# A fused retention and gated feed-forward kernel: two more chunks transposed by the DMA crossbar, and one row of identity products dropped

## The chip, the cores and the metric

The kernel runs on one core of a Trainium2 chip. The metric is the device time of one launch in microseconds (us), as the median of several runs. Times of two kernels are compared within the same rounds on the same chip. A run counts as slow when it is more than 1.5% above the fastest run of the same kernel; only fast runs are compared with fast runs.

## The reference

The program is a retention layer followed by a gated feed-forward layer:

```python
# q, k, v: (4, 8, 768, 64)     (batch, heads, sequence, head size)
for t in range(S):
    state = gamma[None, :, None, None] * state + einsum('bhd,bhe->bhde', k[:, :, t], v[:, :, t])
    y[:, :, t] = scale * einsum('bhd,bhde->bhe', q[:, :, t], state)
x = y.transpose(0, 2, 1, 3).reshape(3072, 512)
out = (1 / (1 + exp(-(x @ w_gate))) * (x @ w_val)) @ w_out      # d_ff = 1536
```

## The kernel before

The kernel cuts the sequence into 24 chunks of 128 positions (four batches of six) and the 3072 tokens into six blocks of 512, four chunks each. For each chunk it makes transposed q and k, the scores of the chunk with itself, a masked product with a scaled v, and the running state. While TensorE works on the feed-forward layer of block t, the attention steps of the four chunks of block t + 1 are placed between its groups of matmuls. All of this is written for a manual schedule: each engine executes its instructions in program order.

The parts that matter here:

```python
XBAR = 12                                    # chunks from 12 on are transposed by the DMA crossbar

def load_kq(g):                              # GpSimd issues the loads (float32 to bfloat16 on the way)
    ...
    nc.gpsimd.dma_start(out=kn[g], in_=src(k, g))
    nc.gpsimd.dma_start(out=qn[g], in_=src(q, g))

def transposes(g):                           # on TensorE: 8 products, and a copy by ScalarE
    tp = pa.tile([128, 2 * NP, C], BF16, tag="tp", name="tp")
    for i, x in enumerate((kn[g], qn[g])):
        for p in range(NP):
            nc.tensor.transpose(tp[:, i * NP + p, :], pair(x, p), ident)
    qkT[g] = at.tile([128, 2 * NP, C], BF16, tag="qkT", name="qkT", bufs=3)
    nc.scalar.activation(qkT[g], tp, AX.Copy)

def xbar(g):                                 # by the DMA crossbar, issued by SyncE: 2 transfers
    qkT[g] = ld.tile([128, 2 * NP, C], BF16, tag="qkX", name="qkX", bufs=8)
    for i, x in enumerate((kn[g], qn[g])):
        nc.sync.dma_start_transpose(out=qkT[g][:, i * NP:(i + 1) * NP, :],
                                    in_=x.rearrange("s h d -> s (h d)"))

def step_t(g):
    if g < XBAR:
        transposes(g)
    scale_v(g, nc.vector if g < 8 else nc.gpsimd)      # from chunk 8 on GpSimd scales v

def step_y(g, nxt=None):
    inter(g)                                 # y  <- state of the chunk before
    if nxt is not None:
        scores(nxt)
    state(g)                                 # z  <- k and scaled v of this chunk
    intra(g)
    ...

def down(t, sm, part):
    ...
    ob = ffn.tile([128, D_MODEL], F32, tag="ob", name="ob")      # pool of 3 buffers
    nc.scalar.copy(ob, o)
    nc.sync.dma_start(out=out[row:row + 128, :], in_=ob)         # stores on SyncE's queue too

def keep_on(n):                              # identity products, only to keep TensorE at work
    u = pf.tile([128, 512], F32, tag="ff", name="ff")
    for _ in range(n):
        nc.tensor.matmul(u[:, :128], ident, ident, start=True, stop=True)

for t in range(NT):
    ...
    if t + 2 < NT:
        for g in range(4 * t + 8, 4 * t + 12):
            load_chunk(g)                    # before this block's scale_v in GpSimd's order
    for i, group in enumerate(groups):
        if i == len(groups) - 9:
            for g in range(4 * t + 8, 4 * t + 12):
                if XBAR <= g < NG:
                    xbar(g)
        group()
        ...                                  # the attention steps placed at this group
```

## Time and profile before

| | before |
|---|---|
| time, median of the first 3 runs | 240.35 us (240.22 to 241.0) |
| span of the profiled run | 238.1 us |
| TensorE busy | 96% |
| granted TensorE clock | 1.00 |
| DMA engines busy | full until about 119 us, then nearly idle |

"PE" is TensorE's matmuls, "PEld" its weight loads, DVE is VectorE, ACT is ScalarE, POOL is GpSimd and SPq the queue of SyncE. A row of slices cuts the span into 40 equal pieces, with the busy share of each in tenths. In the chain of waits each line is a start, a duration and what the end of the program waited for in that time. In a timeline each line is a start, a duration, the engine, the source line and the operation, and in brackets how long the engine was idle before it and what ended that. The lines themselves stand in the prediction.

### The profile page before, as it was taken

To read this page: it belongs to the slowest core of one execution; us is meant where nothing else is said; L and a number is where in the kernel's file an instruction comes from. 1 tells how busy PE (TensorE), PEld (TensorE's weight loads), DVE (VectorE), ACT (ScalarE), POOL (GpSimd) and SP (SyncE) were. 2 spreads that over 40 slices of the span, in tenths; PEclk is the share of its full clock that TensorE was granted. 3 is DMA by queue.
4 is the path that set the end of the run, shared out by engine and by line. 5 is a ranking of instruction groups with operands and counts; after the bars stand their busy time and mean duration, and the time that the engine had idled before them with its cause. 6 is when DMAs were issued, how large, how long until landed. Compare 5 with 4: busy or idle time off the path is not lost.

```text
span 238.1 us, 4313 instructions
## 1 busy us (share of the span) xinstructions
PE 227.8 (96%) x1716; PEld 118.9 (50%) x1742; DVE 102.0 (43%) x172; ACT 90.8 (38%) x169; POOL 95.9 (40%) x114
## 2 busy tenths in 40 slices
PE   7798999999999999999999999999999999999993
PEld 7565644555655554444554445444444554444441
DVE  3467446355545631256641346641346641243300
ACT  7764334425545431234333243223334321334221
POOL 8999874687889346994111001111000000000000
PEclk9999999999999999999999999999999999999999
DMA  7999999999999999999972361012100012100022
GB/s 131 192 189 188 195 205 200 189 212 230 233 169 139 92 138 163 263 175 156 159 110 88 91 104 29 3 45 89 47 0 0 3 44 88 47 0 0 0 88 88
DMA packets 77267, 27.27 MB, mean 115 GB/s; under 512 B 65024, under 2 KB 72704, under 8 KB 77248
## 3 DMA queue, kind: packets, MB, share of 16 engines
q0 software_dynamic: 57616, 16.78, 70.6%
q1 hardware_dynamic: 19632, 10.23, 21.6%
q8 instruction: 13, 0.21, 0.4%
q14 instruction: 6, 0.05, 0.1%
HBM read 28.31 MB, written 6.29 MB: 145 GB/s over the span
## 4 chain that ended last, share of the span: by engine, by line
PE 88%; POOL 6%; issue 2%; ACT 2%; DVE 1%; ACTq 0%; POOLq 0%; DVEq 0%
PE ff L250 49%; PE ff L281 26%; PE sA L168 3%; PE y L204 2%; PE z L190 2%; PE y L180 2%; PE tp L146 2%; POOL vs L158 1%; POOL kn L67 1%; POOL vf L62 1%; POOL qn L68 1%; ACT qkT L148 1%; PE ff L264 1%; ACT ob L286 1%; PE ff L293 1%
## 5 line engine op out<-in xcount | busy, mean ns | idle before, releaser
L255 DVE TENSOR_TENSOR hT<-gs,ff 128x512 bf16<-128x512 f32 (+1 forms) x72 | 48.6, 676 | 75.5 <-PE ff L250 73.9
L250 PE MATMUL ff<-xT,wg 128*128 128x512 bf16 (+1 forms) x276 | 71.5, 375 | 0.9 <-DVE xT L212 0.3
L250 PE MATMUL ff<-xT,wv 128*128 128x512 bf16 (+1 forms) x282 | 71.9, 375 | 0.4
L254 ACT ACTIVATE gs<-ff 128x512 f32<-128x512 f32 (+1 forms) x72 | 42.3, 588 | 68.8 <-PE ff L250 68.3
L281 PE MATMUL ff<-wo,hT 128*128 128x512 bf16 x280 | 65.0, 380 | 0.6 <-issue 0.2
L250 PEld LDWEIGHTS <-wv 128*128 128x128 bf16 x288 | 28.2, 98 | 32.7
L281 PEld LDWEIGHTS <-hT 128*128 128x128 bf16 x288 | 27.0, 98 | 31.6
L250 PEld LDWEIGHTS <-wg 128*128 128x128 bf16 x288 | 26.7, 98 | 30.2 <-issue 0.8
L158 POOL TENSOR_TENSOR vs<-vf,tabv 128x512 bf16<-128x512 f32 x18 | 18.6, 1048 | 47.1 <-PE y L204 42.1
L286 ACT COPY ob<-ff 128x512 f32<-128x512 f32 x24 | 14.0, 585 | 54.3 <-PE ff L281 49.1
L212 DVE TENSOR_TENSOR xT<-y,taby 128x512 bf16<-128x512 f32 x24 | 16.4, 685 | 20.1 <-PE y L204 20.0
L62 POOL DMA_DIRECT2D vf<-in_v_dram x23 | 20.7, 902 | 9.4 <-DMA kn<-in_k_dram 4.7
L173 DVE TENSOR_TENSOR stA<-sA,causal 128x512 bf16<-128x512 f32 x24 | 16.5, 687 | 18.6 <-PE sB L168 18.5
L67 POOL DMA_DIRECT2D kn<-in_k_dram x23 | 20.9, 907 | 7.0 <-DMA qn<-in_q_dram 4.4
L68 POOL DMA_DIRECT2D qn<-in_q_dram x23 | 20.4, 887 | 4.3 <-DMA wo<-in_moe_w_out_dram 2.3
L198 ACT CAST zbd<-z 64x256 bf16<-64x256 f32 x40 | 14.6, 366 | 13.6 <-PE z L190 13.2
L174 DVE TENSOR_TENSOR stB<-sB,causal 128x512 bf16<-128x512 f32 x24 | 16.3, 681 | 0.0
L148 ACT ACTIVATE qkT<-tp 128x1024 bf16<-128x1024 bf16 x12 | 12.3, 1024 | 5.1 <-PE tp L146 5.1
L293 PE MATMUL ff<-ident 128*128 128x128 bf16 x110 | 9.5, 251 | 2.6 <-POOL ident masks.py:199 1.6
L204 PE MATMUL y<-stA,vs 128*64 128x128 bf16 x96 | 9.7, 222 | 0.0
L293 PEld LDWEIGHTS <-ident 128*128 128x128 bf16 x110 | 8.0, 114 | 3.2 <-POOL ident masks.py:199 1.6
L204 PE MATMUL y<-stB,vs 128*64 128x128 bf16 x96 | 9.5, 221 | 0.0
(48 smaller groups left out, 112.9 us busy)
## 6 DMA issues: line engine op xcount, KB each, us to landing
out_dram<-ob SPq DMA_DIRECT2D x24, 256.0 KB, 2.0
vf<-in_v_dram POOLq DMA_DIRECT2D x23, 256.0 KB, 8.6
kn<-in_k_dram POOLq DMA_DIRECT2D x23, 128.0 KB, 8.4
qn<-in_q_dram POOLq DMA_DIRECT2D x23, 128.0 KB, 8.6
wg<-in_moe_w_gate_dram POOLq DMA_DIRECT2D x6, 256.0 KB, 5.8
wv<-in_moe_w_val_dram POOLq DMA_DIRECT2D x6, 256.0 KB, 6.6
wo<-in_moe_w_out_dram POOLq DMA_DIRECT2D x4, 384.0 KB, 11.0
kf<-in_k_dram SPq DMA_DIRECT2D x1, 256.0 KB, 3.4
```

What stands on the lines that cost most here:

```text
L62: eng.dma_start(out=vf[g], in_=src(v, g))
L67: nc.gpsimd.dma_start(out=kn[g], in_=src(k, g))
L68: nc.gpsimd.dma_start(out=qn[g], in_=src(q, g))
L158: eng.tensor_tensor(vs[g], vf[g], tabv[:, g % NCH, :].unsqueeze(2).to_broadcast([C, H, D]), op=ALU.mult)
L173: nc.vector.tensor_tensor(stA[g], sc[g][0], causal4, op=ALU.mult)
L204: nc.tensor.matmul(y[g][i * D:(i + 1) * D, p, :], vs[g][:, 2 * p + i, :], st[:, p, :], start=(first and p == 0), stop=True, skip_group_che ...
L212: nc.vector.tensor_tensor(xT[g // 4][:, :, col:col + C], y[g], taby[:, :, c * C:(c + 1) * C], op=ALU.mult)
L250: nc.tensor.matmul(u[:, lo:hi], w[:, kk, n1 * 128:(n1 + 1) * 128], xT[t][:, kk, lo:hi], start=(kk == 0), stop=(kk == KT - 1))
L254: nc.scalar.activation(gs[:, lo:hi], ps[0][:, lo:hi], AX.Sigmoid)
L255: nc.vector.tensor_tensor(hT[t][:, n1, lo:hi], gs[:, lo:hi], ps[1][:, lo:hi], op=ALU.mult)
L281: nc.tensor.matmul(o, hT[t][:, n1, sm * 128:(sm + 1) * 128], wo[:, n1, :], start=(n1 == 0), stop=(n1 == NFF - 1))
L293: nc.tensor.matmul(u[:, :128], ident, ident, start=True, stop=True)
```

## The change

The intent is to give TensorE, the busiest engine, less to do. The 16 identity products behind the fourth chunk's transposes go, and so do the TensorE transposes of chunks 10 and 11 (with ScalarE's copies). These two chunks are transposed by the crossbar, issued early in block 1.

```diff
-    XBAR = 12
+    XBAR = 10
@@
     transposes(3)
-    keep_on(16)
     scores(3)
@@
         for i, group in enumerate(groups):
-            if i == len(groups) - 9:
-                for g in range(4 * t + 8, 4 * t + 12):
-                    if XBAR <= g < NG:
-                        xbar(g)
+            if t == 1 and i == 2:
+                for g in range(XBAR, 12):
+                    xbar(g)
+            if i == len(groups) - 9 and t > 0:
+                for g in range(4 * t + 8, min(4 * t + 12, NG)):
+                    xbar(g)
             group()
```

## The prediction

> **What bounds the kernel now.** I read the busy table and the slices first, then the chain of waits, then the timelines of single engines where the change acts.
>
> ```profile
> PE 227.8 (96%) x1716; PEld 118.9 (50%) x1742; DVE 102.0 (43%) x172; ACT 90.8 (38%) x169; POOL 95.9 (40%) x114
> PE   7798999999999999999999999999999999999993
> DMA  7999999999999999999972361012100012100022
> PE 88%; POOL 6%; issue 2%; ACT 2%; DVE 1%; ACTq 0%; POOLq 0%; DVEq 0%
> ```
>
> TensorE is busy almost from end to end, so work taken off it is worth its own time, as long as nothing else holds TensorE at that spot. The DMA engines are full for the first half (slices 2 to 20, until about 119 us) and nearly empty after. The chain is TensorE except for a few short stretches; one of them matters here, in the second token block (t = 1), which begins at 57.7 us:
>
> ```profile
> 69.45 0.89 POOL vf L62
> 70.35 1.07 POOL vs L158
> 71.47 0.32 PE z L190 x8
> ```
>
> The chain leaves TensorE for GpSimd: the state product of chunk 8 needs the scaled v of chunk 8, and GpSimd makes that only after it has issued the last load (v of chunk 15) in its program. TensorE waits just 0.15 us for it today, so this spot has no slack.
>
> Is GpSimd there held by its own issuing, or by the transfers? Its timeline:
>
> ```profile
> 32.22 0.90 POOL L67 DMA_DIRECT2D kn<-in_k_dram  x1 [0.56 <-DMA wv<-in_moe_w_val_dram]
> 36.72 0.87 POOL L68 DMA_DIRECT2D qn<-in_q_dram  x1 [0.75 <-DMA wo<-in_moe_w_out_dram]
> ...
> 60.30 0.89 POOL L62 DMA_DIRECT2D vf<-in_v_dram  x1 [0.35 <-issue]
> 83.62 0.87 POOL L67 DMA_DIRECT2D kn<-in_k_dram  x1 [3.63 <-DMA qn<-in_q_dram]
> 88.58 0.89 POOL L62 DMA_DIRECT2D vf<-in_v_dram  x1 [3.21 <-DMA kn<-in_k_dram]
> ```
>
> Counted back in order of issue, the transfer waited for is each time the eighth before (for the load at 32.22 the val weights issued at 23.69; for 83.62 the q load issued at 68.58). So at most eight GpSimd loads are in flight, and the ninth is issued when the first has landed: slower transfers delay GpSimd, and with it everything that stands behind the loads. From 51 to 70 us it issues three loads in about 3.1 us, 1.04 us each, with small gaps of this kind.
>
> SyncE's timeline shows the transposes of the DMA crossbar:
>
> ```profile
> 58.31 0.33 SPq L288 DMA_DIRECT2D out_dram<-ob  x1
> 65.94 1.31 SPq L153 DMA_TRANSPOSE qkX<-kn  x1
> 67.36 2.03 SPq L153 DMA_TRANSPOSE qkX<-qn  x1
> ```
>
> SyncE is free from 58.6 us on and waits 7.3 us for k of chunk 12 to land. The eight transposes of chunks 12 to 15 then run from 65.94 to about 84 us, beside the loads. Their cost to the loads shows in the landing times: the loads of the window 58 to 70 us land in a median of 7.9 to 8.5 us, those of 70 to 90 us in 13.7 to 14.7 us. The transposes themselves take 9.7 to 13.0 us to land there, 2.4 us with no loads about (130 to 155 us).
>
> **What the Trainium skill says.** "DMA: Bandwidth & Descriptors", section "Issuing engines are not separate DMA queues": transfers from all issuing engines run on the same 16 DMA engines and interleave. The trace agrees: landing times nearly double, as just given. The same page, "DMA Transpose (X-bar)": such a transpose can only come from the SyncE or ScalarE queues; here all 24 stand on SyncE's, behind the stores in program order. "TensorE: Matmul & The Clock Gate", "What's actually happening": TensorE idle for about 3.4 us falls to half clock, and needs about 3.4 us of work to come back. The trace has the slow rate only at its start (the first 36 identity products take 4.02 us, 0.11 us each; the 16 at 21.18 us take 1.05 us, about 0.055 us each), and no long idle time after it, so a fall back is not shown.
>
> **Part 1, the 16 identity products.**
>
> ```profile
> 20.22 1.02 ACT L148 ACTIVATE qkT<-tp 128x1024 bf16<-128x1024 bf16 x1 [0.61 <-PE tp L146]
> 21.18 1.05 PE L293 MATMUL ff<-ident 128*128 128x128 bf16 x16 [0.99 <-DVE hT L255]
> 22.16 0.23 PE L168 MATMUL sA<-qkT 64*128 64x128 bf16 x1
> ```
>
> They were to fill the wait for ScalarE's copy, but they wait themselves for a PSUM buffer (0.99 us) and begin at 21.18, when that copy is nearly over (20.22 + 1.02 = 21.24). Without them the scores can start some 0.06 us after the copy (at 62.91 us they start 0.05 us after it), at 21.30 instead of 22.16: **0.86 us earlier**. VectorE ends its two multiplications at 21.58 and is free for the masks. TensorE idles 1.1 us in place of 1.0 us there, too short for the clock. But nothing moves GpSimd earlier, whose load issue does not depend on TensorE here. TensorE arrives at the state product of chunk 8 at 70.45 instead of 71.3 and waits for the same scaled v. I expect the 0.86 us to be **lost there: worth 0**.
>
> **Part 2, chunks 10 and 11 off TensorE.** Each chunk's eight transposes take 0.45 us of the chain (75.57 and 82.32 us), both after the wait at 71.47, where TensorE is the bound with some 5 us of other work between steps: **-0.9 us**. ScalarE's two copies of 1.02 us go too; ScalarE is 38% busy and off the chain: 0.
>
> **Part 3, four more crossbar transposes.** They stand after block 0's stores and before chunks 12 to 15 on SyncE, so the first goes when k of chunk 10 has landed. That load is issued at 51.38; the eighth after it is issued at 60.30 after a short wait, so it lands at about 60.1. Today's first transpose is issued at 65.94: crossbar traffic starts about **5.9 us earlier**. The transposed chunks are in time: with 13 us to land they come by about 79 us, needed at 77.9 (chunk 10, whose two are first, by 75) and 87.2 us (chunk 11). The cost is to the loads. In slices of 1 us, the first crossbar packets appear at 69.6 us, 3.7 us after the issue; so they would appear at about 63.8 us. From then on loads land slower. Today, from 69.6 to 79.0 us, six loads land (q of chunk 13 to k of chunk 15; the eighth load after the last of them is issued at 79.09 after a wait): 1.6 us each against 1.04. For the last load before the scaled v to be issued, k of chunk 13 must have landed, the eighth before it. Of the loads up to it, those issued up to 55.27 have landed by 64.3 us; v of 11, k, q, v of 12 and k of 13 are left, with the rest of one, some six. By today's rate they need 9.4 us: 63.8 + 9.4 = 73.2 in place of about 69.4. So the scaled v comes **3.8 us** later, the state product at about 75.2.
>
> TensorE would then sit idle from 70.45 to 75.2, 4.8 us, over the skill's 3.4 us. If its clock falls, up to 3.4 us run at half rate, a loss of at most 1.7 us; since the trace shows no such case, I count a third of it, 0.5 us (an estimate).
>
> Later blocks have room: the scaled v of chunk 12 is made at 94.38 and used at 107.8, chunk 16's transposes are issued at 97.78 and used at 135.6; some 6 us more of DMA delay fits.
>
> Sum: 0 - 0.9 + 3.8 + 0.5 = +3.4, so 243.75; since the delay is the least certain term and can be smaller, I lower it to **243.0 us**.
>
> **The rivals.**
> A, no new wait: the crossbar takes its turn without slowing GpSimd's issue before 69.45. For it: from 65.94 to 69.45 transposes were issued and the loads did not yet slow; SyncE was idle there. Against: traffic starts 3.7 us after issue and loads slow at once then. It gives -0.9, 239.5; and if the saved 0.86 us counts as well, 238.6.
> B, the wait is larger: the DMA is so disturbed that loads land at 2.0 us each (today 12 loads from 69.2 to 93.3 us), and traffic starts with less lag, so nine loads are left: 9 x 1.0 = 9 us late. With the clock loss and -0.9, about +9: 249.
> C, the transposed chunks 10 or 11 come late themselves, as part of SyncE's row is held by loads: chunk 10 would have to land 17 us after its issue, and the longest today is 13.0. TensorE would wait at the scores of chunk 10 instead, 1 to 3 us, but only where the earlier wait did not already move that use back: little on top.
>
> **Range and chances.** Rival A has some 25%, B's strong form some 8%, the middle (a wait of 2 to 6 us) the rest. That gives 239.2 to 246.8 for 8 in 10. Faster by over 2% needs under 235.5, more than all that is removed: 2%. Slower by over 2% needs over 245.2, a new wait of about 6 us, or 4.5 us with a full clock loss: 15%. Within 2%: 83%.
>
> **What would show it.** Right: the first scores of chunk 3 at about 21.3; transposes on SyncE from about 60 us; the last load before the scaled v issued at 72 to 75 us, TensorE idle 3 to 6 us before the state product of chunk 8, released by the scaled v; from there on each stage as before, less 0.45 us twice. Wrong: the state product still at about 71.4 (A), or the longest new wait elsewhere, at the scores of chunk 10 (C) or in block 2.

## The result

| | before | changed |
|---|---|---|
| median | 240.28 us (239.88 to 241.0) | 247.84 us (246.7 to 248.87) |
| span of the profiled run | 238.1 us | 246.0 us |
| granted clock | 1.00 | 0.979 |

The changed kernel is slower, by a ratio of 1.031 (95% interval 1.026 to 1.036). A ratio here is the mean time of one kernel's fast runs over that of the other's in the same rounds, so it is not quite the ratio of the two medians. The result is correct. 247.84 us lies above the predicted range.

The page of the changed kernel: busy time, slices, and the chain by engine:

```profile
PE 229.7 (93%) x1710; PEld 117.3 (48%) x1710; DVE 102.4 (42%) x172; ACT 88.8 (36%) x167; POOL 95.9 (39%) x114
...
PE   6798999999944999999999999999999999999993
...
PEclk9999999999995799999999999999999999999999
DMA  8999999999999999999999284002200002200022
...
PE 80%; DMA 9%; POOL 5%; ACT 2%; issue 1%; DVE 1%; POOLq 0%; ACTq 0%; DVEq 0%
```

There is now a hole in TensorE's row in slices 12 and 13, and the granted clock falls in slices 13 and 14; DMA transfers, which had no share worth a line in the chain before, hold 9% of it. The timeline of TensorE around the hole:

```profile
21.31 0.23 PE L168 MATMUL sA<-qkT 64*128 64x128 bf16 x1 [1.12 <-ACT qkT L148]
...
77.19 0.42 PE L190 MATMUL z<-vs,kn 128*64 128x64 bf16 x8 [6.74 <-POOL vs L158]
77.98 1.89 PE L250 MATMUL ff<-xT,wg 128*128 128x512 bf16 x4
79.66 1.92 PE L250 MATMUL ff<-xT,wv 128*128 128x512 bf16 x4
81.36 1.80 PE L250 MATMUL ff<-xT,wg 128*128 128x512 bf16 x4
83.00 1.03 PE L250 MATMUL ff<-xT,wv 128*128 128x512 bf16 x4
```

The first line shows that the dropped products did what was expected of them: the scores of chunk 3 start at 21.31 us instead of 22.16. The second is the wait: 6.74 us before the state product of chunk 8, for the scaled v of GpSimd. The next three show groups of four matmuls that start 1.7 us apart, where the fourth and all later ones take 0.87 us: TensorE runs at half clock after the wait. In slices of 0.3 us the clock is 0.50 from about 72.7 us, some 2.2 us after TensorE went idle (at 70.45 us), to about 82.9 us.

The chain of waits in that stretch of the changed kernel, and SyncE's timeline below it:

```profile
62.36 12.26 DMA kn<-in_k_dram
...
75.19 0.89 POOL vf L62
76.09 1.06 POOL vs L158
...
77.19 0.42 PE z L190 x8
...
95.31 10.31 DMA out_dram<-ob
```

```profile
60.66 1.29 SPq L153 DMA_TRANSPOSE qkX<-kn  x1
62.07 1.19 SPq L153 DMA_TRANSPOSE qkX<-qn  x1
63.90 1.50 SPq L153 DMA_TRANSPOSE qkX<-kn  x1
65.50 1.72 SPq L153 DMA_TRANSPOSE qkX<-qn  x1
68.14 1.68 SPq L153 DMA_TRANSPOSE qkX<-kn  x1
```

The load of k of chunk 13, issued at 62.36 us, takes 12.26 us (7.57 before, issued at 61.29). The last load before the scaled v can only be issued when it has landed, at 75.19 us (69.45 before), and the scaled v follows at once. The transposes begin at 60.66 us (65.94 before). The last chain line is a smaller second loss: an output store of block 1 takes 10.31 us to land, and TensorE waits 0.39 us for its buffer (0.55 us from start to start of the matmuls).

Where the time went, read from the start of the state product of each chunk in the two timelines of TensorE:

| state product of chunk | before | changed | later by | what is added |
|---|---|---|---|---|
| 3 | 22.82 | 21.96 | -0.86 | products dropped |
| 8 | 71.47 | 77.19 | +5.72 | the wait (6.74 instead of 0.15, of which 0.86 is the early arrival) |
| 9 | 78.22 | 86.24 | +8.02 | half clock +2.75, chunk 10's transposes -0.45 |
| 10 | 87.57 | 95.14 | +7.57 | chunk 11's transposes -0.45 |
| 12 | 107.72 | 115.84 | +8.12 | the store's buffer +0.55 |
| 22 | 193.99 | 202.12 | +8.13 | nothing |

The spans differ by 7.9 us, the medians by 7.56.

### The profile page after: what moved, and what is told of

It reads as the page before. It is cut to its first block, busy times and chain, and to the rows that moved or that the text cites. A ratio compares the mean times of both kernels' runs of the same rounds, so it can differ in the third digit from the quotient of the medians.

```text
span 246.0 us, 4283 instructions
## 1 busy us (share of the span) xinstructions
PE 229.7 (93%) x1710; PEld 117.3 (48%) x1710; DVE 102.4 (42%) x172; ACT 88.8 (36%) x167; POOL 95.9 (39%) x114
## 4 chain that ended last, share of the span: by engine, by line
PE 80%; DMA 9%; POOL 5%; ACT 2%; issue 1%; DVE 1%; POOLq 0%; ACTq 0%; DVEq 0%
PE ff L250 48%; PE ff L281 22%; DMA kn<-in_k_dram 5%; DMA out_dram<-ob 4%; PE sA L168 2%; PE y L204 2%; PE z L190 2%; PE y L180 2%; POOL vs L158 1%; POOL vf L62 1%; PE tp L146 1%; ACT qkT L148 1%; POOL kn L67 1%; PE ff L264 1%; ACT ob L286 1%
## 5 line engine op out<-in xcount | busy, mean ns | idle before, releaser
L250 PE MATMUL ff<-xT,wg 128*128 128x512 bf16 (+1 forms) x288 | 74.5, 382 | 0.8 <-ACT ob L286 0.4
L250 PE MATMUL ff<-xT,wv 128*128 128x512 bf16 (+1 forms) x288 | 73.6, 379 | 0.0
L190 PE MATMUL z<-vs,kn 128*64 128x64 bf16 x160 | 6.4, 203 | 6.9 <-POOL vs L158 6.9
L148 ACT ACTIVATE qkT<-tp 128x1024 bf16<-128x1024 bf16 x10 | 10.2, 1025 | 3.6 <-PE tp L146 3.6
L293 PE MATMUL ff<-ident 128*128 128x128 bf16 x94 | 8.0, 247 | 1.6 <-POOL ident masks.py:199 1.6
## 6 DMA issues: line engine op xcount, KB each, us to landing
wo<-in_moe_w_out_dram POOLq DMA_DIRECT2D x4, 384.0 KB, 10.4
```

The lines of the kernel that those rows point to most:

```text
L250: nc.tensor.matmul(u[:, lo:hi], w[:, kk, n1 * 128:(n1 + 1) * 128], xT[t][:, kk, lo:hi], start=(kk == 0), stop=(kk == KT - 1))
```

## The experiments

**Theory A.** The whole loss comes from the four earlier crossbar transposes. They slow the loads that are in flight beside them; GpSimd, which keeps at most eight loads in flight, issues its last load later, so the scaled v of chunk 8 comes late; TensorE idles, and its clock falls. **Rivals:** the dropped identity products let the clock fall (C); TensorE waits for the transposed data itself (D); any traffic at that place would do the same.

Unless it says otherwise, an edit is shown against the changed kernel. "Before" in these runs has medians from 240.19 to 240.37 us. The runs e1 to e4, e5 to e8 and e9 to e12 were made on three different chips, so runs of different groups are best compared by their ratios to the kernel before.

### e1_products_dropped: the first part alone

```diff
# against the kernel before
     transposes(3)
-    keep_on(16)
     scores(3)
```

> Only the 16 identity products are dropped; chunks 10 and 11 stay on TensorE. Theory A (the whole loss comes from the four earlier crossbar transposes, which delay the loads and with them GpSimd's scaled v of chunk 8): as the kernel before, 240.3 us within 0.4; scores of chunk 3 at about 21.3 us, and TensorE waits about 1.0 us instead of 0.15 before the state product of chunk 8, which still starts at about 71.4 us. Rival B (the saved 0.86 us counts): 239.4 us. Rival C (the products kept the TensorE clock up, and their loss is what slows the changed kernel): slower than 242 us, with a granted clock under 1.00.

240.35 us, ratio 1.000 (0.998 to 1.002). In its timeline of TensorE:

```profile
71.90 0.32 PE L190 MATMUL z<-vs,kn 128*64 128x64 bf16 x8 [1.44 <-POOL vs L158]
```

TensorE comes 0.86 us earlier and waits until 71.90 us. GpSimd's gate swallows the saving, and the clock stays at 1.00. Rivals B and C of that list are out.

### e2_products_kept: the change without its first part

```diff
     transposes(3)
+    keep_on(16)
     scores(3)
```

> The changed kernel with the 16 identity products put back. Theory A: as slow as the changed kernel, 247.8 us within 0.8; the wait before the state product of chunk 8 is about 5.9 us (6.7 less the 0.86), and it ends at the same time, about 77 us; the clock still falls behind it. Rival C (the dropped products are the cause): back to about 239.5 us.

248.27 us, ratio 1.033 (1.029 to 1.038): as slow as the changed kernel. In the profiled run the wait is 7.71 us and ends at 79.04, rather later than expected; its time is 249.03. The runs fall into two pairs by clock, 249.03 and 249.75 us at 0.979, 247.5 and 246.9 us at 0.986. These steps can be read: in the profiled runs the stretches at half clock last 3.4 us (0.993: e3_spare_transposes, e8_plain_copies) or 10.2 us (0.979: the changed kernel, and this one), so by estimate 0.986 is two times 3.4 us. The products are not the cause.

### e3_spare_transposes: the added traffic alone

```diff
# against the kernel before; nobody reads the spare tiles
         for i, group in enumerate(groups):
+            if t == 1 and i == 2:
+                for g in range(10, 12):
+                    spare = ld.tile([128, 2 * NP, C], BF16, tag="spare", name="spare", bufs=2)
+                    for j, x in enumerate((kn[g], qn[g])):
+                        nc.sync.dma_start_transpose(out=spare[:, j * NP:(j + 1) * NP, :],
+                                                    in_=x.rearrange("s h d -> s (h d)"))
```

> The kernel before, with products and TensorE transposes of chunks 10 and 11 as they were, and the four crossbar transposes of these chunks added into spare tiles that nobody reads. Theory A: the added traffic alone makes the loss, 248.7 us within 1.0 (the changed kernel's 247.8 plus the 0.9 us of TensorE transposes that stay). Rival D (the loss comes from waiting for the transposed data of chunks 10 and 11): 240.3 us, since nobody waits for it.

248.3 us, ratio of the fast runs 1.030 (1.025 to 1.035); one of the four runs is slow (250.89 us, at the clock of 0.979 that three of the changed kernel's fast runs have). All computing is as in the kernel before, and no one waits for the added transfers, yet the loss is there. In the profiled run, the fastest of the four (245.59 us), the scaled v begins at 74.72 us and the wait is 4.52 us. Rival D is out: the traffic is enough.

### e4_no_transposes_wrong: the saving alone

Wrong result (relative error 0.50): chunks 10 and 11 read chunk 9's transposed tile.

```diff
         if g < XBAR:
             transposes(g)
+        elif g < 12:
+            qkT[g] = qkT[9]
@@
             if t == 1 and i == 2:
-                for g in range(XBAR, 12):
-                    xbar(g)
+                pass
```

> Wrong result on purpose: the changed kernel without any transpose of chunks 10 and 11 (they read chunk 9's transposed tile). Theory A: no added traffic, so the state product of chunk 8 starts at about 71.4 us; the TensorE transposes saved count, 2 x 0.45 us: 239.4 us within 0.4. If they did not count: 240.3 us. If dropping the products or the transposes were itself harmful: over 242 us.

239.55 us, five of the six runs between 239.38 and 239.79; the ratio is 0.998 (0.995 to 1.002) because the sixth took 241.68 at a clock of 0.993, by the estimate above one stretch of 3.4 us at half clock. Without the added traffic the wait in the profiled run is 1.57 us and the clock 1.00. By the medians about 0.8 us are saved, near the 0.9 expected, though the interval of the ratio includes no saving.

### e7_kept_busy: the clock by itself

```diff
             scores(nxt)
+        if g == 8:
+            keep_on(104)
         state(g)
```

> The changed kernel with 104 identity products (about 5.8 us at full clock) put in front of the state product of chunk 8, into the wait of 6.7 us. Theory A with the clock as second term: the wait ends when it did, about 77 us, but the three groups of matmuls behind it run at 0.87 us instead of 1.7, so 2.4 to 2.7 us less than the changed kernel: 245.3 us, granted clock 1.00. If the slow groups behind the wait had another cause (the crossbar's traffic): 247.8 us as before.

245.73 us, ratio 1.023 (1.018 to 1.028), clock 0.999 to 1.000 in all four runs. Its timeline of TensorE (the edit moves line numbers up by two):

```profile
70.36 5.98 PE L295 MATMUL ff<-ident 128*128 128x128 bf16 x104
78.05 0.32 PE L190 MATMUL z<-vs,kn 128*64 128x64 bf16 x8 [1.71 <-POOL vs L158]
78.52 1.04 PE L252 MATMUL ff<-xT,wg 128*128 128x512 bf16 x4
79.40 1.03 PE L252 MATMUL ff<-xT,wv 128*128 128x512 bf16 x4
```

The wait ends no earlier (78.05 us), but the groups behind it start 0.87 us apart at once. The crossbar's traffic is the same, so the slow groups of the changed kernel are the clock's, not the traffic's. It saves 2.1 us by the medians; the intervals of the two ratios touch (1.018 to 1.028, and 1.026 to 1.036), so the timeline is the stronger evidence.

### e8_plain_copies: plain copies in place of the spare transposes

```diff
# against e3_spare_transposes
-   nc.sync.dma_start_transpose(out=spare[:, j * NP:(j + 1) * NP, :],
-                               in_=x.rearrange("s h d -> s (h d)"))
+   nc.sync.dma_start(out=spare[:, j * NP:(j + 1) * NP, :].rearrange("s p c -> s (p c)"),
+                     in_=x.rearrange("s h d -> s (h d)"))
```

> As the run with four spare crossbar transposes, but each is a plain copy of the same bytes between the same places (128 rows of 1 KB, no transposing). Theory A in the form that the many small packets of a transpose cost (about 548 packets of under 512 B each, against some 144 here): little delay, 240.3 to 241.3 us. Rival (any transfer of these bytes at that time costs as much): about 248 us.

243.32 us, ratio 1.012 (1.010 to 1.015): between the two, so both expectations miss. The scaled v begins at 71.95 us, 1.6 us later than before; in e3_spare_transposes it was 4.4 us later. So plain copies delay the loads as well, in these two profiled runs by about a third as much as transposes of the same bytes. The start of the scaled v also varies without any added traffic, so the landing time of k of chunk 13 is the cleaner measure: 7.5 to 7.6 us in the profiled runs without added transfers or with two transposes (before, e1, e4, e10, e11), 9.1 us here, and 11.4 to 15.7 us in the eight with four transposes. Why the loss of some 3 us is more than the delay shows in the timeline of TensorE:

```profile
73.06 0.32 PE L190 MATMUL z<-vs,kn 128*64 128x64 bf16 x8 [1.76 <-POOL vs L158]
73.53 1.47 PE L250 MATMUL ff<-xT,wg 128*128 128x512 bf16 x4
74.80 1.91 PE L250 MATMUL ff<-xT,wv 128*128 128x512 bf16 x4
```

A wait of only 1.76 us was enough for the clock to fall, 0.9 us after work had begun again (it is at half from about 74.0 to 77.4 us).

### e11_only_chunk_11: half of the added transposes

```diff
-    XBAR = 10
+    XBAR = 11
```

> The changed kernel with the crossbar for chunk 11 alone (two added transposes instead of four, and the first about 3 us later). Theory A: the scaled v of chunk 8 comes 1.5 to 2.5 us later than in the kernel before, TensorE waits about 3 us, the clock falls for one to two stretches of 3.4 us (1.2 to 2.4 us lost), and 0.45 us are saved: 243.4 us, 242 to 245. If the loss does not depend on the number of transposes: 247.8 us; if it only begins with the fourth: 240 us.

239.85 us, ratio 0.998 (0.996 to 1.000): a miss for theory A's size, there is no loss at all; of the alternatives only the last (240 us) fits. Its first added transpose waits for k of chunk 11 and is issued at 63.79 us, 3.1 us after the changed kernel's. The load that counts, k of chunk 13, was issued at 62.13 us and lands in time for the last load at 70.20; the scaled v begins at 71.10, 0.75 us later than before, hardly more than in e4_no_transposes_wrong, which adds no traffic (0.67). TensorE waits 1.75 us, the clock stays, and the 0.45 us saved roughly pay for the rest. So the loss is not proportional to the number of transposes. The trace suggests that it depends on how many of the loads up to k of chunk 13 are still under way when the crossbar's traffic begins (here at 66.3 us by the packets, against 63.7 in the changed kernel). But this run changes the number and the start at once, so which of the two counts is not shown.

### e5_v_on_vector and e6_loads_behind_v: opening GpSimd's gate

Two ways to free the scaled v of chunk 8 from the loads in front of it: VectorE makes it, or GpSimd issues six of those loads later.

```diff
# e5_v_on_vector
-        scale_v(g, nc.vector if g < 8 else nc.gpsimd)
+        scale_v(g, nc.vector if g < 12 else nc.gpsimd)
```

> The changed kernel with the scaled v of chunks 8 to 11 made by VectorE, which has no loads to issue in front of it. Theory A (the crossbar transposes hurt only through GpSimd, whose scaling stands behind the held-up load issues): the wait before the state product of chunk 8 and the fall of the clock vanish, and both savings count, 240.3 - 0.9 - 0.86 = 238.6 us, 238.2 to 239.4. Rival (the crossbar slows TensorE or the data of chunks 8 to 11 in another way too, so that a wait for transposed or loaded data takes its place): over 241 us.

```diff
# e6_loads_behind_v
-            for g in range(4 * t + 8, 4 * t + 12):
+            for g in range(4 * t + 8, 4 * t + (10 if t == 1 else 12)):
                 load_chunk(g)
@@
+            if t == 1 and i == 3:
+                for g in (14, 15):
+                    load_chunk(g)
             group()
```

> The changed kernel with GpSimd's order changed: the loads of chunks 14 and 15 are issued after the scaled v of chunk 8, so six loads fewer stand in front of it. Theory A: the scaled v of chunk 8 comes by about 67 us, before its use at 70.5, the clock stays at 1.00, and the time is 238.6 us, 238.2 to 239.4, as with VectorE. If some later scaled v (chunk 9 at about 77 us) is now held by the loads behind: 240 to 244 us, with the wait at the state product of chunk 9.

Both miss. e5_v_on_vector: the four fast runs lie between 245.86 and 247.41 us, ratio 1.026 (1.023 to 1.029); two runs are slow, the profiled one among them (250.06). e6_loads_behind_v: only two runs are fast, 243.28 and 243.44, ratio 1.012 (1.009 to 1.015); the profiled one is slow (249.36). In both profiles the wait at chunk 8 is gone, and a new one has taken its place, for an output buffer. The waits of TensorE of e5_v_on_vector (total, count, longest), and the chain in front of that wait:

```profile
PE ff L250 <- ACT ob L286: 10.4, 1, 10.4
```

```profile
70.22 20.61 DMA kn<-in_k_dram
...
90.84 1.19 SPq L153
...
92.13 1.35 SPq L153
...
93.57 12.42 DMA out_dram<-ob
...
106.08 0.59 ACT ob L286
...
106.72 3.57 PE ff L250 x8
```

This is a second gate. The output stores of block 1 stand behind the transposes of chunk 15 in SyncE's queue, those wait for k of chunk 15, and that load takes 20.61 us to land. So no store is issued before 93.57 us, although ScalarE had written the first buffer by 85.7 us; the store takes 12.42 us, all three output buffers are full, ScalarE waits 14.10 us, and TensorE gets no free PSUM buffer. In the changed kernel TensorE came there 9.6 us later (the first buffer was written at 95.3 us), so this gate cost only 0.39 us. In e6_loads_behind_v the same wait is 5.1 us, and 2.5 us more go to the scaled v of chunk 9 behind the moved loads. Since both profiles are of slow runs, the size of these waits is not the size of the fast runs' loss; the next run tests the gate itself.

### e12_vector_12_stores_8: both gates opened

```diff
# against e5_v_on_vector
-        ob = ffn.tile([128, D_MODEL], F32, tag="ob", name="ob")
+        ob = ffn.tile([128, D_MODEL], F32, tag="ob", name="ob", bufs=8)
```

> The changed kernel with the scaled v of chunks 8 to 11 on VectorE, as in the earlier run, and eight output buffers as the only further edit. Theory A2: the wait of 10.4 us for an output store goes, and with it the fall of the clock: 238.6 to 239.5 us (a wait of about half a us for the scaled v of chunk 12, which GpSimd still makes behind its loads, may stay). Rival (that wait is for the transfers themselves and only moves): over 244 us.

237.92 us, ratio 0.992 (0.989 to 0.994), a little under the expected 238.6 to 239.5. One edit of the number of buffers takes 8 to 9 us off e5_v_on_vector. The waits for output buffers are gone; what is left in the profiled run (239.09 us, the slowest of the six) is 1.25 us, for the scaled v of chunk 12, which GpSimd still makes behind its loads.

### e9_vector_16_stores_8: the fastest version

```diff
# against the changed kernel
-        scale_v(g, nc.vector if g < 8 else nc.gpsimd)
+        scale_v(g, nc.vector if g < 16 else nc.gpsimd)
@@
-        ob = ffn.tile([128, D_MODEL], F32, tag="ob", name="ob")
+        ob = ffn.tile([128, D_MODEL], F32, tag="ob", name="ob", bufs=8)
```

> The changed kernel with the scaled v of chunks 8 to 15 on VectorE and eight output buffers instead of three. Theory A2 (two gates in row: GpSimd's scaling behind the held-up loads, and then SyncE's stores of block 1, which stand behind transposes that wait for late loads until the three output buffers run out): with both gates opened, no wait of TensorE over 1.2 us is left after 25 us, clock 1.00, and the removed work counts: 240.3 - 0.9 - 0.86 = 238.6 us, 238.0 to 239.3. Rival (a third gate behind these: loads or transposed data of chunks 12 to 15 too late): over 240 us, with the wait named there.

237.53 us (237.51 to 237.88), ratio 0.989 (0.988 to 0.991): faster than both kernels, with a correct result. It is 1.1 us under the expected time and below the expected range. All waits of TensorE over 0.25 us (total, count, longest):

```profile
PE sA L168 <- ACT qkT L148: 2.1, 4, 1.1
PE ff L293 <- POOL ident masks.py:199: 1.6, 1, 1.6
PE z L190 <- POOL vs L158: 0.4, 1, 0.4
PE ff L250 <- DVE xT L212: 0.3, 1, 0.3
```

After the first 22 us only 0.3 us of them is left, one wait for ScalarE's copy that the kernel before has as well. The state product of chunk 22 starts at 192.02 us, 1.97 us before that of the kernel before: 0.86 of the products, 0.9 of the transposes, and 0.15 of the old wait. The rest of the difference in medians (2.66 us) is partly scatter of the kernel before, whose eleven runs here reach from 239.58 to 240.82 us while its traced run is at 239.81.

### e10_same_without_crossbar: what the crossbar part is worth with open gates

```diff
# against e9_vector_16_stores_8
-    XBAR = 10
+    XBAR = 12
```

> As the run before it in this list, but chunks 10 and 11 stay on TensorE (no added crossbar transposes; identity products dropped, v on VectorE to chunk 15, eight output buffers). Theory A2: only the 0.86 us of the products count, which GpSimd's gate had swallowed: 239.4 us, 238.9 to 239.9, so 0.9 us more than with the crossbar. If the products' 0.86 us is lost at another wait: 240.3 us.

238.66 us, ratio 0.994 (0.992 to 0.996), 0.2 us under the expected range. The order is as expected: with the gates open the dropped products count (e1_products_dropped had shown 0 for them), and the crossbar adds another 1.13 us by the medians. Since this run also moves v and adds buffers, the trace is the check: the state product of chunk 22 starts at 192.92 us, 1.07 us before that of the kernel before (0.86 + 0.15 explain 1.01) and 0.90 us after that of e9_vector_16_stores_8.

## Why the prediction was right or wrong

**The waits named were right.** The spot (state product of chunk 8), its releaser (the scaled v behind the loads), the number of loads in flight, and the order of events up to the state product were seen as predicted. Part 1 was right: the scores start at 21.31 us (21.30 predicted), and alone the part is worth 0.00 +- 0.5 us (e1_products_dropped). Part 2 was right in size, -0.45 us at each of two steps in the table above; the pair e9_vector_16_stores_8 and e10_same_without_crossbar agrees (0.90 us in the traces), and the medians of e4_no_transposes_wrong are near it. Transposed data was in time, as rival C of the prediction was given little.

**The term of the delay was too small.** The step that failed reads: "By today's rate they need 9.4 us: 63.8 + 9.4 = 73.2 in place of about 69.4. So the scaled v comes 3.8 us later, the state product at about 75.2." The start of the traffic was right: the first packets of the new transposes appear at 63.7 us. But k of chunk 13 landed only at 74.62 us (the chain's 62.36 + 12.26), so the six loads took 1.8 us each, not 1.6; and 0.57 us more passed until the next load was issued, where the working adds nothing: it took the landing of k of chunk 13 in the kernel before for 69.4 us, which is the issue that follows (the trace has the landing at 68.85). In the same way k of chunk 10 landed there at 59.45 us and not at 60.1. The state product came at 77.19 us, 5.72 us later than before instead of 3.7. The estimate took the rate from a stretch of the kernel before in which GpSimd issued no loads for 4 us while it scaled four tiles; in the new place loads were issued all along. That this pause made the old rate milder is an argument, not shown by a run. The delay also varies from run to run: the scaled v began at 76.09 us in the changed kernel, at 77.94 in e2_products_kept and at 74.72 in e3_spare_transposes. And not all of it is the crossbar's: in the changed kernel's profile k of chunk 13 was issued 1.07 us later than before (62.36 against 61.29), when the new transposes had moved no packet yet; in e1, e4 and e10, which add no transposes, it was 0.5 to 1.3 us later. The larger part is its landing, 4.7 us longer. Lowering the sum from 243.75 to 243.0, because the delay "can be smaller", went the wrong way too.

**The term of the clock was much too small.** The step reads: "I count a third of it, 0.5 us (an estimate)." It measured 2.75 us from the state product of chunk 8 to that of chunk 9, and 2.1 us by the medians of e7_kept_busy. The fall did not last one stretch of 3.4 us, as the 1.7 us assumed, but three: 10.2 us, of which TensorE had work for 5.7. In the sum, 5.72 + 2.75 - 0.9 + 0.55 = 8.1, against the profile's 7.9. These two terms were 4.3 in the working; they are 8.5.

**What the prediction did not see.** SyncE's queue as a second gate was not named, except as "the longest new wait elsewhere"; "Later blocks have room" had checked the scaled v and the transposes, but not the stores. In the changed kernel it costs 0.39 us, so it does not explain the miss; but it hid behind the first and took over when that was opened (e5_v_on_vector, shown by e12_vector_12_stores_8). The strong form of rival B, 249 us at 8%, is nearest in the total, but by luck: it had nine loads left and the scaled v 9 us late, where six were left and it came 5.74 us late, and the clock made up the rest. The middle form (a wait of 2 to 6 us) came close for the wait, 6.74 us; what took the time over the range is the clock. Rival A's loss-free course is what half of the transposes show (e11_only_chunk_11).

**Left open.** Why transposes hold up the loads more than plain copies of their bytes (k of chunk 13 lands 3.8 to 8.1 us later after its issue with the one, 1.5 us with the other) was not taken apart. Eight output buffers without the scaled v on VectorE were not run. From what idle time on the clock falls could not be fixed either (last section).

## What to carry to other kernels

Work moved from a busy engine to the DMA must be checked against what is in flight at that moment: an engine that issues loads and also computes in program order passes every delay of a transfer on to its computing. An idle stretch of TensorE costs its length and can cost again in clock (6.74 us of wait lost 2.75 us more here, one of 1.76 us lost some too, four of 1.44 to 1.75 us nothing), so a wait of some us should be counted with both. When a gate is opened, look for the next in-order queue behind it; here the scaled v on VectorE alone left the kernel 2.6% slower, and together with more output buffers it turned the change from 3% slower to 1% faster.

## What the Trainium skill lacked or had wrong

- "TensorE: Matmul & The Clock Gate", section "What's actually happening", puts the fall of the clock after at least one idle window of about 3.4 us. Here it fell 2.2 us after TensorE went idle in the changed kernel (70.45 to 72.7 us), but 5.3 us after in e3_spare_transposes (71.3 to 76.6). In e8_plain_copies it fell after a wait of only 1.76 us, at 74.0 us, when TensorE was already at work again for 0.9 us; waits of 1.44, 1.57, 1.71 and 1.75 us (e1_products_dropped, e4_no_transposes_wrong, e7_kept_busy, e11_only_chunk_11, profiled runs) left it at 0.998 to 1.00. So idle time well short of the page's window can be enough, and 1.75 us kept the clock where 1.76 us lost it: the length of the wait alone does not decide, and where the limit lies these runs do not settle.
- The same section gives at least one busy window of about 3.4 us for the clock to come back. The runs agree, but only as a least time: it took 5.7 us of work at half clock in the changed kernel (77.19 to 82.9 us) and 3.4 us in e8_plain_copies. The stretches at half clock were 10.2 and 3.4 us long, so multiples of the window that the page gives; an estimate from one window, as in the prediction, was too small.
- "DMA: Bandwidth & Descriptors", "Issuing engines are not separate DMA queues", says that transfers interleave, but no page says by how much crossbar transposes slow loads beside them. Here four of them (eight follow) took the loads issued between 58 and 70 us from a median of 7.9 to 8.5 us to landing to 11.3 to 13.8 us, and a transpose itself, 2.4 us with no loads about, took 6.5 to 14.2 us among them.
- No page draws the consequence for a store that stands in one issuing queue behind a transpose which waits for its own input: in e5_v_on_vector no output was issued until 93.57 us, with the first ready at 85.7, and TensorE lost 10.4 us (a profile of a slow run).
